# Two attentions and two gated layers in one kernel: where the weights between the attentions are placed, and how much of V and of the gate and up weights stays resident

## The chip, the cores and the metric

The kernel runs on one core of a Trainium2 chip. The metric is device time in microseconds, the median of several executions. One execution more was taken by the hardware profiler; its trace is what the readings below come from.

## The reference

The program computes four layers in a row on a tiny batch: four sequences, one token each, model width 512. Attention A and gated layer B are each applied twice, with the same weights and the same cache both times:

```python
def _A_ref(x, k_cache, v_cache, wq, wo):
    W = min(4096, max(256, Sk // 4))                    # 2048 of 8192 positions
    q = (x @ wq) ...                                    # 32 heads of 128
    k = jnp.repeat(k_cache[:, :, Sk - W:, :], 4, axis=1)   # 8 heads in the cache
    v = jnp.repeat(v_cache[:, :, Sk - W:, :], 4, axis=1)
    p = _softmax(einsum(q, k) * Dh ** -0.5)
    return einsum(p, v) ... @ wo

def _B_ref(x, w_gate, w_up, w_down):
    return (_sigmoid(x @ w_gate) * (x @ w_up)) @ w_down    # 512 -> 1792 -> 512

x = x + _A_ref(_layernorm(x), ...)     # layer 0
x = x + _B_ref(_layernorm(x), ...)     # layer 1
x = x + _A_ref(_layernorm(x), ...)     # layer 2
x = x + _B_ref(_layernorm(x), ...)     # layer 3
```

All arrays are bfloat16. K and V of one cache head (all four sequences, 2048 positions) are 2 MB each, 32 MB for both and all eight heads. The query and output weights are 4 MB each, gate, up and down 1.75 MB each.

## The kernel before

**Memory.** The on-chip memory is counted in *units* of 256 bfloat16 columns, 64 KB over the 128 partitions. K or V of one head is 32 units, a quarter of a gate or up matrix (128 of the 512 rows) is 7 units, the query weights are 64, four blocks of the down weights are 8. There are these buffers: `kt` (K of all heads, 256 units), `wo_sb` (output weights, 64 units, called "ws" in the table of places), `arena` ("ar", 75 units), `side` ("sx", 31 units), and the small `qs`, `pb`, `pt`. K and the output weights are loaded once and serve both attentions. Half of the query weights stays in `side` and at the end of `arena`. V is streamed in both attentions, but the pieces that still lie in `arena` from the first attention are not loaded again: `VKEEP` names, for a head, the first unit of the piece that is kept.

**Places.** The dictionary `WHERE` says for each load where it lands: `V0_h` and `V2_h` are V of head h in the first and second attention, `u01`, `g23_1` and so on pairs of quarters of up and gate (`_1` and `_3` is the layer), `d4_1` the down weights from block 4 on, `q01` the streamed half of the query weights. A load into a place where something else lay waits until the last reader of that has finished. Nothing else holds it back.

**Order.** A planner lists all operations with their data dependences, then orders each engine's by its own list of costs. SyncE (SP) issues all loads, in the order in which the program lists them; one that waits holds up all behind it. The other engines take ready operations, with a preference for those listed first. So when places change, the order of operations on TensorE, VectorE and ScalarE may change with them. The engines wait on one another by semaphores.

**The stages.** In the first attention each head's K is transposed on TensorE (L740), the scores are computed (L763), a maximum over them is taken (L772), exponentials are made on ScalarE (L785), transposed on VectorE (L791) and by a permuting matmul (L796), spread into a block form (L821 on VectorE, L828 on ScalarE), multiplied with V (L863 for a wide form whose partial sums are then added in L879, L921 for a narrow one), selected by row (L961, L968) and multiplied with the output weights (L988). Six TensorE steps, two ScalarE steps and up to nine VectorE steps per head follow one another. The second attention does the same without the transposes of K. It computes scores two heads ahead of the product with V. V of its heads 2 to 7 goes into `kt`, where K of heads 0 to 6 was, as soon as the scores of these heads are done.

Between the attentions stands layer 1: up and gate (L1157), the sigmoid on ScalarE, down (L1233), then the norm and the query projection of layer 2 (L703). Part of the output weights is meanwhile moved into the accumulators ("stash", L1036) and back (L1031), so that `wo_sb` has room for streamed weights. Layer 3 is the same as layer 1 with another form of the down product (L1230); then the output is written.

The quarters of gate and up are multiplied in the order up 0, up 1, gate 0 to 3, up 2, up 3, which `glu` writes out; the blocks of the down weights of layer 1 in the order 0, 4, 7, 8, 10, 12 (the first block of each piece).

Of the kernel before, what the change touches and what calls it, by code (L numbers as in the profile page):

```python
# [268 lines left out]
def build(nc, A_x, A_k, A_v, A_wq, A_wo, B_wg, B_wu, B_wd, out):  # L269
# [4 lines left out]
    _, HKV, SK, DH = A_k.shape  # L274
# [4 lines left out]
    NC = D // 128  # L279
    F = B_wg.shape[1]  # L280
    NFC = F // 128
# [16 lines left out]
    UHEAD = NB * UBLK  # L298
    KEEPG = 4
    GU = F // UNIT  # L300
# [6 lines left out]
    WIDE = {0: {0: 4, 1: 4, 2: 4, 3: 4, 4: 4, 5: 4, 6: 2}, 2: {2: 2, 3: 2, 4: 2, 5: 2}}  # L307
    VKEEP = {0: 24, 7: 19}
    HEADS1 = list(range(1, HKV - 1)) + [0, HKV - 1]
# [29 lines left out]
    with es:  # L339
# [81 lines left out]
        MAIN = WKEEP[2][0][1]  # L421
        G0 = MAIN - KEEPG * GU
# [618 lines left out]

        def load_g(L, nm, ktc, keep):
            key = (nm, ktc // 2, 0 if keep or (nm, ktc // 2, 0) in gkeep else L)
            if key not in gkeep:
                s = WHERE["%s%d%d" % (nm, key[1] * 2, key[1] * 2 + 1) + ("_%d" % L if key[2] else "")]
                gkeep[key] = s
                dma("w%s%d_%d" % (nm, L, ktc), blk_ap(s), (wg_d if nm == "g" else wu_d)[:, key[1], :], w=blk_tok(s),
                    rate="bw_7k")
            s = gkeep[key]
            return (s[0], s[1] + ktc % 2 * GU, GU)  # L1050
# [85 lines left out]
        def glu(L, last_layer):  # L1136
# [9 lines left out]
            wid = NB if last_layer else NB + 1  # L1146
            for nm, ktc in (("u", 0), ("u", 1), ("g", 0), ("g", 1), ("g", 2), ("g", 3), ("u", 2), ("u", 3)):
                bank = GB if nm == "g" else UB
                keep = not last_layer and 2 * ktc + (nm == "u") < KEEPG
                s = load_g(L, nm, ktc, keep)  # L1150

                def e_g(pe, ktc=ktc, s=s, bank=bank):
                    last = None
                    for fc in range(NFC):
                        g0, gn = WD[fc // 4]
                        cols = blk_ap(s)[:, g0 * 128:(g0 + gn) * 128].rearrange("p (m j) -> p j m", j=gn)
                        last = pe.matmul(ps[:, bank, fc * wid:(fc + 1) * wid],  # L1157
                                         cols[:, fc - g0, :],
                                         xn[:, ktc * (NB + 1):ktc * (NB + 1) + wid],
                                         start=(ktc == 0 and fc == 0), stop=(ktc == NC - 1),  # L1160
                                         skip_group_check=True)
# [53 lines left out]
            if not last_layer:  # L1215
                parts[1:] = [(4, 7), (7, 8), (8, 10), (10, 12), (12, 14)]
            for fc0, fc1 in parts:
                s = load_d(L, fc0, fc1)

                def e_d(pe, fc0=fc0, fc1=fc1, s=s):  # L1220
                    last = None
                    src = blk_ap(s)
                    for fc in range(fc0, fc1):
                        for c in range(NC):
# [3 lines left out]
                            if last_layer:  # L1228
                                f0 = fc // 7 * 32 + fc % 7
                                last = pe.matmul(ps[32 * c:32 * c + 25, YB, 0:128], hS[:, f0:f0 + 25], wd,  # L1230
                                                 start=False, stop=(fc == NFC - 1), skip_group_check=True)
                            else:
                                last = pe.matmul(ps[:, YB, c * NB:(c + 1) * NB], wd, hf,  # L1233
                                                 start=(fc == 0 and c == 0), stop=(fc == NFC - 1),
                                                 skip_group_check=True)
# [188 lines left out]
```

## Time and profile before

| what | value |
|---|---|
| time, three executions | 174.51 us median, 174.02 to 175.1 |
| the profiled execution | 174.79 us, of which the profile's span is 173.05 |
| mean granted TensorE clock | 0.82 |
| TensorE busy | 136.2 us, 79% of the span, 2179 matmuls |
| VectorE busy | 100.7 us, 58% |
| ScalarE busy | 77.3 us, 45% |
| read from HBM | 68.62 MB, 397 GB/s over the span |
| first attention, layer 1 and query projection, second attention, layer 3 | to about 106, to 124, to 162, to 173 us |

Times in the profile are microseconds from the start of the span. A row of the timeline has the start, the duration, the engine, the line of the kernel, the operation, the operands as out<-in, their shapes and the count; brackets hold the idle time of the engine ahead of the row and what ended it. "us to landing" of a transfer is counted from its issue by SyncE. Where a text says that a transfer lands at some time, it is the sum of both.

### The profile page before, as it was taken

To read this page: it belongs to the slowest core of one execution; us is meant where nothing else is said; L and a number is where in the kernel's file an instruction comes from. 1 tells how busy PE (TensorE), PEld (TensorE's weight loads), DVE (VectorE), ACT (ScalarE), POOL (GpSimd) and SP (SyncE) were. 2 spreads that over 40 slices of the span, in tenths; PEclk is the share of its full clock that TensorE was granted. 3 is DMA by queue.
4 is the path that set the end of the run, shared out by engine and by line. 5 is a ranking of instruction groups with operands and counts; after the bars stand their busy time and mean duration, and the time that the engine had idled before them with its cause. 6 is when DMAs were issued, how large, how long until landed. Compare 5 with 4: busy or idle time off the path is not lost.

```text
span 173.0 us, 4894 instructions
## 1 busy us (share of the span) xinstructions
PE 136.2 (79%) x2179; PEld 100.4 (58%) x2179; DVE 100.7 (58%) x252; ACT 77.3 (45%) x134; POOL 8.0 (5%) x19
## 2 busy tenths in 40 slices
PE   0395589899898779998979676657977989689883
PEld 0292388658466458565655366546625756458772
DVE  7535015886848675795797653113279877754450
ACT  2064207848576646566291230110767463554200
POOL 5200000000000000000000000202200000000020
PEclk9999756999999987999999755555569999956755
DMA  5999999999999999999999999999999999999960
GB/s 183 424 422 411 432 424 428 439 409 449 424 416 433 400 445 424 412 427 428 420 417 418 397 419 416 406 400 411 386 385 452 426 420 405 424 416 423 407 250 5
DMA packets 9361, 68.93 MB, mean 398 GB/s; under 512 B 1017, under 2 KB 1917, under 8 KB 6013
## 3 DMA queue, kind: packets, MB, share of 16 engines
q1 hardware_dynamic: 9332, 68.62, 95.7%
q8 instruction: 17, 0.28, 0.6%
q14 instruction: 4, 0.02, 0.0%
q10 hardware_dynamic: 8, 0.00, 0.0%
HBM read 68.62 MB, written 0.00 MB: 397 GB/s over the span
## 4 chain that ended last, share of the span: by engine, by line
DMA 65%; PE 23%; DVE 6%; ACT 2%; issue 2%; SPq 1%; DVEq 0%; ACTq 0%
DMA arena<-in_A_v_cache_dram 32%; DMA kt<-in_A_k_cache_dram 12%; DMA kt<-in_A_v_cache_dram 10%; DMA wo_sb<-in_B_w_down_dram 7%; PE ps L863 5%; PE ps L740 4%; DMA wo_sb<-in_A_wq_dram 4%; PE ps L763 3%; PE ps L1157 2%; PE ps L921 2%; SPq L464 1%; DVE pt L821 1%; PE ps L1230 1%; PE ps L836 1%; PE ps L988 1%
## 5 line engine op out<-in xcount | busy, mean ns | idle before, releaser
L750 ACT COPY kt<-ps 128x1024 bf16<-128x1024 bf16 x40 | 39.2, 1017 | 28.2 <-PE ps L740 28.0
L740 PE MATMUL ps<-ident_r,kt 128*128 128x128 bf16 x512 | 40.4, 238 | 5.1 <-DMA kt<-in_A_k_cache_dram 3.1
L740 PEld LDWEIGHTS ps<-ident_r,kt 128*128 128x128 bf16 x512 | 34.9, 109 | 11.8 <-issue 4.4
L750 DVE COPY kt<-ps 128x1024 bf16<-128x1024 bf16 x24 | 29.1, 1214 | 14.2 <-PE ps L740 14.0
L763 PE MATMUL ps<-kt,qs 128*32 128x512 bf16 x256 | 18.3, 413 | 1.2 <-ACT pb L785 1.2
L821 DVE TENSOR_TENSOR pt<-ps,ofbr 128x1024 bf16<-128x1024 f32 (+1 forms) x15 | 15.4, 1029 | 2.7 <-PE ps L796 2.7
L863 PE MATMUL ps<-arena,pt 128*64 128x512 bf16 (+1 forms) x128 | 13.1, 377 | 3.0 <-DMA arena<-in_A_v_cache_dram 3.0
L772 DVE TENSOR_REDUCE nmz<-ps 128x1 f32<-128x512 f32 x16 | 11.0, 688 | 5.9 <-PE ps L763 5.8
L791 DVE STREAM_TRANSPOSE pb<-pb 128x512 bf16<-128x512 bf16 x16 | 11.3, 704 | 4.2 <-ACT pb L785 4.1
L785 ACT ACTIVATE pb<-ps,nmz 128x512 bf16<-128x512 f32 x16 | 11.1, 692 | 5.8 <-DVE nmz L782 5.8
L828 ACT ACTIVATE pt<-ps,ofbr 128x96 bf16<-128x96 f32 x28 | 7.2, 342 | 7.8 <-PE ps L796 7.8
L863 PEld LDWEIGHTS ps<-arena,pt 128*64 128x64 bf16 (+1 forms) x128 | 5.9, 111 | 7.9 <-DMA arena<-in_A_v_cache_dram 4.0
L763 PEld LDWEIGHTS ps<-kt,qs 128*32 128x32 bf16 x256 | 5.8, 101 | 7.8 <-ACT pb L785 2.2
L872 ACT COPY arena<-ps 128x512 f32<-128x512 f32 (+1 forms) x7 | 3.9, 555 | 11.9 <-PE ps L863 11.7
L1031 ACT COPY wo_sb<-ps 128x1024 bf16<-128x1024 bf16 x5 | 5.0, 1011 | 9.1 <-PE ps L703 9.1
L836 PE MATMUL ps<-rowf,nmz 128*128 128x16 f32 x32 | 6.9, 292 | 2.7 <-DVE pt L821 2.5
L836 PEld LDWEIGHTS ps<-rowf,nmz 128*128 128x128 f32 x32 | 5.4, 212 | 5.8 <-DVE pt L821 4.2
L1157 PE MATMUL ps<-xn,arena 128*128 128x5 bf16 (+1 forms) x168 | 6.3, 172 | 2.2 <-DMA arena<-in_B_w_up_dram 1.1
L634 POOL TENSOR_TENSOR rs<-pt,rs 128x4 f32<-128x4 f32 x3 | 3.0, 1014 | 106.0 <-DVE pt L630 106.0
L879 PEld LDWEIGHTS ps<-arena 128*128 128x128 f32 x52 | 6.7, 201 | 2.1 <-ACT arena L872 1.6
L879 PE MATMUL ps<-arena 128*128 128x16 f32 x52 | 7.4, 273 | 0.6
L1157 PEld LDWEIGHTS ps<-xn,arena 128*128 128x128 bf16 x168 | 6.3, 118 | 2.5 <-DMA arena<-in_B_w_up_dram 1.2
(170 smaller groups left out, 162.9 us busy)
## 6 DMA issues: line engine op xcount, KB each, us to landing
kt<-in_A_k_cache_dram SPq DMA_DIRECT2D x8, 2048.0 KB, 24.6
arena<-in_A_v_cache_dram SPq DMA_DIRECT2D x7, 2048.0 KB, 20.2
kt<-in_A_v_cache_dram SPq DMA_DIRECT2D x3, 2048.0 KB, 14.9
wo_sb<-in_A_wo_dram SPq DMA_DIRECT2D x8, 512.0 KB, 25.1
kt<-in_A_v_cache_dram SPq DMA_DIRECT2D x4, 1024.0 KB, 19.3
kt<-in_A_wq_dram SPq DMA_DIRECT2D x1, 2048.0 KB, 11.7
side<-in_A_wq_dram SPq DMA_DIRECT2D x1, 1984.0 KB, 15.8
arena<-in_B_w_up_dram SPq DMA_DIRECT2D x2, 896.0 KB, 8.0
```

The source lines that it names most:

```text
L740: last = pe.transpose(bankb(bank)[:, (v * NB + q) * 128:(v * NB + q + 1) * 128], kt[:, c0:c0 + 128], ident_b[:, :])
L750: return (e.tensor_copy if ev == "vector" else e.copy)(to, fr)
L763: last = pe.matmul(ps[32 * b:32 * b + 32, sbk, 0:CB * 128], qs[:, q0:q0 + 32], blk_ap(kblk(h, b))[:, c * CB * 128:(c + 1) * CB * 128], sta ...
L772: lambda v: v.tensor_reduce(nmv, ps[:, sbk, 0:CB * 128], AXX, ALU.max, negate=True),
L785: o = a.activation(pbuf[:, :], ps[:, sbk, 0:CB * 128], ACTF.Exp, bias=gv, scale=1.0, accum_out=zv)
L791: P.op("vector", "ptr%d_%d" % (L, h), 650.0, lambda v: v.transpose(turned[:, :], pbuf[:, :]), r=[("pb", 0), ("pb", 1)], w=[("pb", 2), ("pb ...
L821: lambda v: v.tensor_tensor(pv4[:, 0:nj], spread(tbk, nj).unsqueeze(2).broadcast_to([128, nj, NB, REP]), ofb[:, :].unsqueeze(1).unsqueeze( ...
L828: last = a.mul(pv4[:, nj:NJ4, b, :], spread(MB, NJ4 - nj), ofb[:, b:b + 1])
L836: lambda pe: pe.matmul(ps[:, tbk, CB * NQ:CB * NQ + NR], zv.broadcast_to([128, 128]), rowf[:, :], start=True, stop=True),
L863: last = pe.matmul(ps[rows * g:rows * (g + 1), bank, 0:wide * 128].rearrange("p (c d) -> p c d", c=wide), ptv[:, w0:w0 + rows], v, start=( ...
L879: last = pe.matmul(ps[:, out[0], out[1]:out[1] + NR], part[:, c * 128:(c + 1) * 128], ey[wide][:, c * NR:(c + 1) * NR], start=(c == 0), st ...
L1157: last = pe.matmul(ps[:, bank, fc * wid:(fc + 1) * wid], cols[:, fc - g0, :], xn[:, ktc * (NB + 1):ktc * (NB + 1) + wid], start=(ktc == 0 ...
```

## The change

The change gives other places to the weights that stand between the attentions, and to what is kept.

- Of V, head 0 keeps 24 units (before 8) and head 7 keeps 15 (before 13), 39 together. Head 0's second attention loads one piece of 8 units into `side`, in place of four pieces. Of gate and up, the quarters up 0, up 1 and gate 1 stay resident (21 units; before also gate 0, 28). Layer 3 loads gate 0 again, as a load of its own.
- In layer 1, up 2 and up 3 are loads of their own. Up 3 is placed where gate 2 was, the first four down blocks where gate 3 was, the down blocks from 6 on where gate 0 was; the streamed query weights are placed where up 2, up 3, down pieces 0 and 4, and down piece 6 with part of gate 0 were. In each case the load waits for TensorE's reading of what lay there.
- The quarters of layer 1 are multiplied in the order up 0, up 1, gate 2, 3, 0, 1, up 2, up 3; the down pieces in the order 4, 8, 0, 10, 12, 6. The loads of pieces 4 and 8 are issued ahead of that of up 3.

```diff
-    KEEPG = 4
+    KEPTG = {("u", 0), ("u", 1), ("g", 1)}
...
-    VKEEP = {0: 24, 7: 19}
+    VKEEP = {0: 8, 7: 17}
...
-        WHERE["V0_%d" % (HKV - 1)] = [ar(0, 19), ar(23, 13)]
-        WHERE["u01"], WHERE["g01"] = ar(52, 2 * GU), ar(38, 2 * GU)
+        WHERE["V0_%d" % (HKV - 1)] = [ar(15, 17), ar(0, 15)]
+        WHERE["u01"], WHERE["g01"] = ar(36, 2 * GU), ar(22, 2 * GU)
         PT3 = ("kt", 187, 4)
         WHERE.update({
-            "g23_1": ("ws", 8, 2 * GU), "u23_1": ar(0, 2 * GU),
-            "d0_1": ar(14, 8), "d4_1": ("ws", 22, 6), "d7_1": ar(36, 2), "d8_1": ("qs", 0, 4), "d10_1": ("pb", 0, 4),
-            "d12_1": ("pt", 4, 4),
-            "q01": [("ws", 8, 10), ar(0, 14), ("ws", 18, 8)],
-            "V2_0": [ar(14, 9), ar(36, 2), sx(0, 8), sx(8, 5), ar(66, 8)],
-            "V2_1": [sx(13, NS - 13), ar(0, 14)],
+            "g23_1": ("ws", 8, 2 * GU), "u2_1": ar(15, GU), "u3_1": ("ws", 8, GU),
+            "d4_1": ("ws", 24, 4), "d8_1": ("qs", 0, 4), "d10_1": ("pb", 0, 4), "d12_1": ("pt", 4, 4),
+            "d0_1": ("ws", 15, 8), "d6_1": ar(22, 4),
+            "q01": [ar(15, 7), ("ws", 8, 7), ("ws", 15, 13), ar(24, 5)],
+            "V2_0": [sx(0, 8), ar(50, 24)],
+            "V2_1": [sx(8, NS - 8), ar(15, 9)],
             "V2_6": [("kt", 128, 16), ("kt", 144, 16)],
-            "V2_7": [("kt", 160, 12), ("kt", 172, 7), ar(23, 13)],
-            "g23_3": ar(0, 2 * GU), "u23_3": sx(0, 2 * GU),
-            "d0_3": ar(14, 8), "d4_3": ("kt", 192, 8), "d8_3": ("kt", 200, 8), "d12_3": sx(14, 4),
+            "V2_7": [("kt", 160, 10), ("kt", 170, 7), ar(0, 15)],
+            "g0_3": ("kt", 0, GU), "g23_3": ar(15, 2 * GU), "u23_3": sx(0, 2 * GU),
+            "d0_3": ("kt", 8, 8), "d4_3": ("kt", 192, 8), "d8_3": ("kt", 200, 8), "d12_3": sx(14, 4),
         })
...
-            for nm, ktc in (("u", 0), ("u", 1), ("g", 0), ("g", 1), ("g", 2), ("g", 3), ("u", 2), ("u", 3)):
+            turn = [("u", 0), ("u", 1)] + [("g", a) for a in ((1, 0, 2, 3) if last_layer else (2, 3, 0, 1))] + [("u", 2), ("u", 3)]
+            early_d = {}
+            for at, (nm, ktc) in enumerate(turn):
...
+                if not last_layer and (nm, ktc) == ("u", 3):
+                    early_d.update((a, load_d(L, a, a + 2)) for a in (4, 8))
...
-                parts[1:] = [(4, 7), (7, 8), (8, 10), (10, 12), (12, 14)]
+                parts = [(4, 6), (8, 10), (0, 4), (10, 12), (12, 14), (6, 8)]
```

On TensorE the new plan moves, in the second attention, the scores of head 7 behind the product of head 4 with V, and the probabilities of head 6 and the partial sums of head 4 ahead of the first half of head 5's product. On the other engines the same operations follow in a like order; on ScalarE the copy of head 5's partial sums comes ahead of the exponentials of head 7 instead of behind them.

More of the change, by code (lines that the diff above doesn't have):

```diff
@@ L421, in build @@
         MAIN = WKEEP[2][0][1]
-        G0 = MAIN - KEEPG * GU
         def ar(u, n):
@@ L1040, in build, with load_g @@
         gkeep = {}
-        def load_g(L, nm, ktc, keep):
-            key = (nm, ktc // 2, 0 if keep or (nm, ktc // 2, 0) in gkeep else L)
+        def load_g(L, nm, ktc):
+            kept = (nm, ktc) in KEPTG
+            name = "%s%d_%d" % (nm, ktc, L)
+            if not kept and name in WHERE:
+                s = WHERE[name]
+                dma("w" + name, blk_ap(s), (wg_d if nm == "g" else wu_d)[:, ktc // 2, ktc % 2 * F:(ktc % 2 + 1) * F], w=blk_tok(s),
+                    rate="bw_4k")
+                return s
+            key = "%s%d%d" % (nm, ktc // 2 * 2, ktc // 2 * 2 + 1) + ("" if ktc < 2 else "_%d" % L)
+            s = WHERE[key]
             if key not in gkeep:
-                s = WHERE["%s%d%d" % (nm, key[1] * 2, key[1] * 2 + 1) + ("_%d" % L if key[2] else "")]
                 gkeep[key] = s
-                dma("w%s%d_%d" % (nm, L, ktc), blk_ap(s), (wg_d if nm == "g" else wu_d)[:, key[1], :], w=blk_tok(s),
-                    rate="bw_7k")
-            s = gkeep[key]
+                dma("w" + key, blk_ap(s), (wg_d if nm == "g" else wu_d)[:, ktc // 2, :], w=blk_tok(s), rate="bw_7k")
             return (s[0], s[1] + ktc % 2 * GU, GU)
@@ L1146, in glu, with e_g @@
             wid = NB if last_layer else NB + 1
-            for nm, ktc in (("u", 0), ("u", 1), ("g", 0), ("g", 1), ("g", 2), ("g", 3), ("u", 2), ("u", 3)):
+            turn = [("u", 0), ("u", 1)] + [("g", a) for a in ((1, 0, 2, 3) if last_layer else (2, 3, 0, 1))] + [("u", 2), ("u", 3)]
+            early_d = {}
+            for at, (nm, ktc) in enumerate(turn):
                 bank = GB if nm == "g" else UB
-                keep = not last_layer and 2 * ktc + (nm == "u") < KEEPG
-                s = load_g(L, nm, ktc, keep)
-                def e_g(pe, ktc=ktc, s=s, bank=bank):
+                first, end = ktc == turn[0 if nm == "u" else 2][1], ktc == turn[-1 if nm == "u" else 5][1]
+                if not last_layer and (nm, ktc) == ("u", 3):
+                    early_d.update((a, load_d(L, a, a + 2)) for a in (4, 8))
+                s = load_g(L, nm, ktc)
+                def e_g(pe, ktc=ktc, s=s, bank=bank, first=first, end=end):
                     last = None
@@ L1159, in e_g @@
                                          xn[:, ktc * (NB + 1):ktc * (NB + 1) + wid],
-                                         start=(ktc == 0 and fc == 0), stop=(ktc == NC - 1),
-                                         skip_group_check=True)
+                                         start=(first and fc == 0), stop=end, skip_group_check=True)
                     return last
@@ L1215, in glu @@
             if not last_layer:
-                parts[1:] = [(4, 7), (7, 8), (8, 10), (10, 12), (12, 14)]
+                parts = [(4, 6), (8, 10), (0, 4), (10, 12), (12, 14), (6, 8)]
             for fc0, fc1 in parts:
-                s = load_d(L, fc0, fc1)
+                s = early_d[fc0] if fc0 in early_d else load_d(L, fc0, fc1)
                 def e_d(pe, fc0=fc0, fc1=fc1, s=s):
@@ L1233, in e_d @@
                                 last = pe.matmul(ps[:, YB, c * NB:(c + 1) * NB], wd, hf,
-                                                 start=(fc == 0 and c == 0), stop=(fc == NFC - 1),
+                                                 start=(fc == parts[0][0] and c == 0), stop=(fc == parts[-1][1] - 1),
                                                  skip_group_check=True)
```

## The prediction

> **What bounds the kernel now.** I read the page's busy lines and slices first, then the chain, the table of windows, the timelines of TensorE and SyncE, and the rows of DMA issues.
>
> The slices of the page:
>
> ```profile
> ## 2 busy tenths in 40 slices
> ...
> PEclk9999756999999987999999755555569999956755
> DMA  5999999999999999999999999999999999999960
> ...
> HBM read 68.62 MB, written 0.00 MB: 397 GB/s over the span
> ## 4 chain that ended last, share of the span: by engine, by line
> DMA 65%; PE 23%; DVE 6%; ACT 2%; issue 2%; SPq 1%; DVEq 0%; ACTq 0%
> ```
>
> The DMA engines are full in every slice but the first and the last two, and 65% of the chain is transfers. So bytes matter. But in order of time the chain leaves the transfers at 149.9 us (V of head 5, first half) and stays on TensorE, VectorE and ScalarE to the end: the last 23 us are computing. Whether fewer bytes shorten the end is therefore decided in the second attention. Its windows:
>
> ```profile
> core 0: us, PE busy (x) PEld busy (x) DVE busy (x) ACT busy (x) POOL busy (x), PEclk, DMA share, GB/s
> ...
> 135.21:138.62 3.41, 3.39 (x91) 2.36 (x79) 2.98 (x12) 1.75 (x7) 0.00 (x0) 1.00 0.97 413
> ...
> 142.03:145.45 3.42, 3.06 (x62) 1.95 (x62) 2.34 (x9) 1.95 (x7) 0.00 (x0) 1.00 0.97 410
> 145.45:148.87 3.42, 3.07 (x64) 1.97 (x63) 3.33 (x11) 1.87 (x7) 0.54 (x2) 1.00 0.99 414
> 148.87:152.28 3.41, 1.96 (x30) 1.46 (x30) 1.90 (x7) 1.52 (x6) 0.00 (x0) 1.00 1.02 425
> 152.28:155.69 3.41, 2.96 (x28) 1.91 (x28) 1.88 (x5) 1.70 (x7) 0.00 (x0) 0.50 0.99 409
> ```
>
> The first figures are the window and TensorE's busy time; the last three are granted clock, DMA share and rate. TensorE is full to about 142, has gaps to 152.3, and then is granted half its clock. The gaps, in TensorE's timeline:
>
> ```profile
> 142.57 1.06 PE L863 MATMUL ps<-kt,pt 128*32 128x256 bf16 x32 [0.36 <-DMA kt<-in_A_v_cache_dram]
> ...
> 147.49 1.06 PE L863 MATMUL ps<-kt,pt 128*32 128x256 bf16 x32 [0.35 <-DMA kt<-in_A_v_cache_dram]
> 148.37 0.39 PE L988 MATMUL ps<-wo_sb,onr 128*16 128x512 bf16 x4
> ...
> 149.99 0.62 PE L863 MATMUL ps<-kt,pt 128*32 128x256 bf16 x16 [0.90 <-DMA kt<-in_A_v_cache_dram]
> ...
> 152.58 0.60 PE L988 MATMUL ps<-wo_sb,onr 128*16 128x512 bf16 x4 [0.32 <-DVE onr L968]
> ```
>
> Three products with V (heads 3, 4 and the first half of 5) wait for their transfer: 0.36 + 0.35 + 0.90 = 1.61 us. Earlier products don't: V of head 2 lands at 125.92 + 11.5 = 137.4 and is used at 139.0. The same output projection takes 0.39 us at full clock and 0.60 after 152.28.
>
> **Bytes.** A unit is 256 columns, 64 KB. Kept V grows from 8 + 13 to 24 + 15 units, so V of head 0 loads 8 instead of 24 and V of head 7 loads 17 instead of 19. Kept gate and up fall from 28 to 21, so the second gated layer loads 7 more. Net 11 units, 0.72 MB. Heads 3 and 4 are issued at 127.63 and 129.41 and land 14.9 and 18.0 later, 142.5 and 147.4: 4.9 us for 32 units, 0.153 each. So from V of head 1 to V of head 6 everything lands 16 × 0.155 = 2.5 us earlier, V of head 7 2.8, and the last down weights 1.75 earlier (150.28 + 18.8 = 169.1 becomes 167.3).
>
> **The weights between the attentions.** Up, gate, down and query weights up to the second attention are 116 units before and after, so the last query weights still land at 116.54 + 6.9 = 123.4 if SyncE's queue never runs dry. This is where waits are added, each on a read by TensorE. SyncE issues in order, so everything later stands behind the waiting load. What counts is the lead: how long after the issue the transfer ahead of it lands. Before:
>
> ```profile
> 95.29 0.54 SPq L464 DMA_DIRECT2D arena<-in_A_v_cache_dram  x1
> ...
> 98.89 0.34 SPq L464 DMA_DIRECT2D arena<-in_B_w_up_dram  x1
> ...
> 116.54 0.33 SPq L464 DMA_DIRECT2D wo_sb<-in_A_wq_dram  x1
> ```
>
> V of head 7 is issued at 95.29 and lands 8.3 later, 103.6; the up weights were issued at 98.89, so their lead is 4.7 us, the smallest there. After the change the leads are:
> - up 0/1 stand where sums of head 0 lay. Those are read until 99.32 + 1.03 = 100.35: lead 3.2.
> - gate 0/1 and up 2 wait for head 7's first 34 products, 103.3; gate 2/3 ahead lands at 108.0: lead 4.7.
> - up 3 takes gate 2's place, read at about 109.4 (TensorE ran 42 such matmuls in 108.26 to 109.75, right behind the norm). Ahead are gate 0/1 (110.2), up 2 (111.3) and two down pieces of 0.7 each (112.7): lead 3.2. Behind it stand all other down pieces and the query weights.
> - the query pieces wait for up 2, up 3, the 8-unit down piece and the last down piece. That last one is read at 118.8, as now (row at 118.42, 0.38 long): leads 3.8 to 5.
> - V of heads 0 and 1 wait for the query matmuls in the side buffer, 119.7 and 121.0: leads 3.7. V of head 2 is issued at 125.9 as now: lead 4.0 instead of 6.6.
>
> A dry queue costs the latency of one transfer less the lead. That latency lies between 2.1 us (the output, issued at 170.92, span end 173.05) and 2.7 (first K, 7.6 us to landing less 4.9 for its bytes). All leads are above 2.7, so I take 0. Bounds: nothing, and, if the two leads of 3.2 fell short by half a microsecond each, +1.0. What hides these waits is the queue's backlog.
>
> The other edits I cost at nothing. The matmuls are the same, only head 0's kept columns come first in its product. From V of head 7 to the output there are 37 issues in both versions. Rows get shorter in places: up 2/3, one load of 14 units with 7 KB rows, becomes two of 7 units with 3.5 KB. The nearest row is V of head 7's second piece, 7 units of 3.5 KB rows, which lands at 142.23 + 18.2 = 160.4, 1.1 us behind its first piece (141.65 + 17.6): 0.16 a unit, as the wide ones. Bounds: nothing to 0.2 for all of them.
>
> **TensorE's path.** Until the product of head 3 nothing waited for V, so it starts at about 142.2 instead of 142.57 whatever lands earlier. From there the order changes: the scores of head 7 (1.05 us at 145.76) move from before the product of head 4 to behind it, and the probabilities of head 6 and the sums of head 4 come before the first half of head 5. With V there, the first half of head 5 ends 1.1 us earlier (if waits for VectorE of 0.3 to 0.5, like those at 151.74 and 152.58, take the place of part of the three) to 1.6 (if none do). I take 1.5, nearer to the row of the three waits, because work that filled no gap now fills them. Next, the second half of head 5 (1.07 at half clock, from 152.97) and its output projection (0.60) would run ahead of 152.28, at 0.55 and 0.39. That is 0.7 less; the exponentials and transposes of head 7 (0.69 + 0.71) are now the partner they wait for, and hide part. I take 0.5; bounds 0, and 1.3 if the busier windows keep the full clock up to the last product as well. Sum on the path: −1.5 − 0.5 = −2.0.
>
> A limit from the transfers: V of head 7 lands at 160.4 − 2.8 = 157.6, and from there to the end of its output projection it takes 162.2 − 160.4 = 1.8, so 159.4. TensorE's path gives 160.2 and decides. Behind it the second gated layer takes 162.2 to 170.9 as now, 8.7 us, and its last down weights (167.3) are there before they are read (168.0 and later). So all of the −2.0 reaches the end.
>
> The span was 173.05 and its run 174.79; after, 171.05 and 172.79. That run is 0.28 above the median of the three, 174.51. Against the median: **172.5 us**.
>
> On the clock, the Trainium skill's page "TensorE: Matmul & The Clock Gate" (Part 1: The HAM clock gate) says that the clock is either half or full, and goes by how busy TensorE was in free-running windows of about 3.4 us. The windows above agree: 1.96 of 3.41 us busy was followed by 0.50, 3.07 by 1.00. By that rule the fuller window at 148.9 would leave the clock at full rate; the rival below prices it from rows.
>
> **The rivals.**
> - The clock falls as before, or a little earlier, and VectorE's chain replaces the waits: only 1.1 is gained, 173.4. For it: the window of 148.87 gets the shorter matmuls too and stays near the limit. Chance 0.26.
> - The clock stays full to the last product. 155.69 to 159.10 was all busy at half clock; without that, and with the −2.0, TensorE would pass the transfers' limit, so the limit holds: 159.4, −2.8, 171.7. Chance 0.14.
> - Transfers are hidden anyway: TensorE at 99% in 135 to 138.6 is the bound, and freed waits turn into waits for VectorE (busy 3.33 of 3.42 in 145.45 to 148.87). Only the 0.36 before head 3 goes: 174.2. Chance 0.08.
> - Slower: the queue runs dry between the attentions. Place: up 3 and the pieces behind it, whose places come free only when TensorE has read them. From the query weights to head 3 computing has no slack, so a delay there reaches the end in full. It decides as soon as 123.4 becomes later than 125.4. With three leads short by 1.2 each, 3.6 − 2.0 = +1.6, 176.1. Against it: leads over 3. Chance 0.10.
>
> My forecast, 171.9 to 172.9, has 0.42.
>
> **How the numbers follow.** About 1% (1.75 us, bound at 172.76) is what a measurement of this kernel can tell from no change. Faster: four fifths of the forecast's 0.42, the full-clock case's 0.14, a tenth of 0.26: 0.50. Slower: 0.10. The rest, 0.40, is within 1%. The range goes from the full-clock case less 0.8 for cheaper transfers, 170.9, to 174.7, which takes in the hidden case and a queue that is dry for two microseconds; beyond lie the rest of the slower case and little else.
>
> **What would show it.** HBM read 67.90 MB. Up 3 issued near 109.4 and no gap of SyncE after which a landing comes over 1 us late. Query weights landed by 123.4, scores of head 0 from 124.0. No wait of L862 on V in the second attention; PE clock full until at least 152. The output issued near 168.9. I am wrong if the scores start later than 125, or if TensorE's gaps before the products stay, now put down to VectorE.

## The result, and the profile after

The changed kernel is slower. Its median is 175.56 us, that of the kernel before in the same session 174.42; the ratio is 1.0068 with a 95% interval of 1.0047 to 1.0090, so 1.2 us more. The forecast was 172.5, in a range of 170.9 to 174.7. The profiled execution took 175.99 us with a span of 174.15.

The slices, the bytes and the chain on the page of the changed kernel:

```profile
PEclk9999855999999999999999855555567899995555
DMA  5999999999999999999999999998999999999960
...
HBM read 67.90 MB, written 0.00 MB: 390 GB/s over the span
## 4 chain that ended last, share of the span: by engine, by line
DMA 48%; PE 31%; DVE 12%; ACT 3%; issue 2%; SPq 1%; DVEq 0%; ACTq 0%
```

The bytes are what was forecast, 0.72 MB fewer. But slice 28 of the DMA row is no longer full, the rate over the span fell from 397 to 390 GB/s, and the transfers' share of the chain fell from 65% to 48%: TensorE's went from 23% to 31% and VectorE's from 6% to 12%. SyncE's issues behind up 3, in its timeline, and two rows of DMA issues (KB, and us from issue to landing) for the last two query pieces:

```profile
109.06 0.33 SPq L463 DMA_DIRECT2D wo_sb<-in_B_w_up_dram  x1
...
115.74 2.04 SPq L463 DMA_DIRECT2D wo_sb<-in_A_wq_dram  x2
118.71 0.33 SPq L463 DMA_DIRECT2D arena<-in_A_wq_dram  x1
```

```profile
wo_sb<-in_A_wq_dram SPq DMA_DIRECT2D x1, 832.0 KB, 6.8
arena<-in_A_wq_dram SPq DMA_DIRECT2D x1, 320.0 KB, 6.4
```

The second row of the timeline is two loads, the second and the third query piece. The third (13 units) had to wait until the down product had read piece 0, and was issued at 117.46. The piece ahead of it landed at 120.45, so its lead was 2.99 us. It landed at 117.46 + 6.8 = 124.28, which is 3.83 behind the piece ahead; 13 units need 2.05 at the rate of full slices. So 1.8 us of transfers were lost there. The last piece landed at 125.08 (before 123.41). The windows show the hole, first in the changed kernel, then in the kernel before:

```profile
core 0: us, PE busy (x) PEld busy (x) DVE busy (x) ACT busy (x) POOL busy (x), PEclk, DMA share, GB/s
...
118.00:120.00 2.00, 1.47 (x49) 1.34 (x47) 0.88 (x5) 0.00 (x0) 0.10 (x1) 0.50 0.89 249
120.00:122.00 2.00, 1.89 (x57) 1.80 (x54) 1.07 (x6) 0.00 (x0) 0.36 (x2) 0.50 0.80 310
122.00:124.00 2.00, 0.36 (x14) 0.27 (x11) 0.00 (x0) 1.01 (x1) 0.85 (x1) 0.50 0.92 327
```

```profile
118.00:120.00 2.00, 1.45 (x49) 1.28 (x46) 0.88 (x5) 0.00 (x0) 0.55 (x1) 0.50 1.00 408
120.00:122.00 2.00, 1.89 (x57) 1.81 (x55) 1.06 (x6) 0.00 (x0) 0.26 (x2) 0.50 1.03 409
122.00:124.00 2.00, 1.64 (x57) 1.51 (x57) 0.49 (x2) 1.69 (x2) 0.94 (x1) 0.50 1.04 369
```

The last column is the rate, the one ahead of it the DMA engines' busy share. I call *hole* what is short of 410 GB/s over the five windows of 2 us from 116 to 126, in us of transfer: 2.0 after, 0.2 before. The difference, 1.8 us, is as much as 0.72 MB take (1.75). The saving was spent before the second attention began. A hole is not all idle time: by the shares of the three windows (0.89, 0.80, 0.92 against 1.00 to 1.04) the engines stood idle for about 0.9 us of it, and in the rest they were busy with packets that took longer, by their records in the trace: those of the third query piece took up to 2.1 us each, where the median was 0.25. TensorE's timeline of the changed kernel, and then two rows of the kernel before:

```profile
115.10 0.61 PE L1165 MATMUL ps<-xn,wo_sb 128*128 128x5 bf16 x14 [3.04 <-DMA wo_sb<-in_B_w_up_dram]
...
124.33 0.85 PE L702 MATMUL ps<-xn,wo_sb 128*128 128x4 bf16 x26 [1.97 <-DMA wo_sb<-in_A_wq_dram]
...
125.96 3.56 PE L762 MATMUL ps<-kt,qs 128*32 128x512 bf16 x32 [0.41 <-DVE pt L715]
...
133.35 1.90 PE L762 MATMUL ps<-kt,qs 128*32 128x512 bf16 x16 [0.51 <-ACT pb L784]
...
144.38 0.83 PE L762 MATMUL ps<-kt,qs 128*32 128x512 bf16 x12 [1.10 <-issue]
```

```profile
123.46 0.59 PE L703 MATMUL ps<-xn,wo_sb 128*128 128x4 bf16 x16 [0.36 <-DMA wo_sb<-in_A_wq_dram]
123.98 3.60 PE L763 MATMUL ps<-kt,qs 128*32 128x512 bf16 x32
```

In the changed kernel it waits 3.04 us for up 3 (which makes the down product, and so the third query piece, late), then 1.97 us for that query piece. The scores of head 0 start at 125.96 (before 123.98). The scores of head 3 run at half clock (1.90 instead of 1.05), and within those of head 5 there is a stall of 1.10. None of the products of L862 waits for V. The output is issued at 172.01, before 170.92.

A second profiled execution of each kernel was taken to see what of this is of the kernel.

> The changed kernel once more, for a second profiled execution. What belongs to the kernel comes again: up 3 issued near 109, the third query piece issued near 117.5 and landing after 123.8, the scores of head 0 at 125.5 to 126.5, no wait for V before head 6. If the half clock at the scores of head 3 (1.90 us instead of 1.05) and the stall of 1.10 us inside the scores of head 5 belong to it too, the output is issued near 172; if they are chance of one execution, one or both are missing and it is issued near 170.5 to 171.2.

> The kernel before once more, for a second profiled execution: scores of head 0 at 123.9 to 124.5, V of head 2 landing near 137.5, of head 7 near 160.4, waits of TensorE for V ahead of the products of heads 3, 4 and 5 of 1.0 to 1.8 us together, and the output issued at 170.2 to 170.9 (the median run is 0.5 us shorter than the profiled one).

The changed kernel took 175.91. Third query piece issued at 117.77 with a lead of 3.02, last query weights at 126.13, scores at 126.53, half clock at the scores of head 3 again, output issued at 172.03. The stall inside head 5's scores did not come again, and yet the output was no earlier. V of head 7 landed at 161.38, and its output projection ended 1.73 behind that, the same step from transfers to the end as the 1.8 of before. In the first execution V of head 7 had landed at 160.72 and the projection ended 3.11 behind it: there computing was the later of the two. The kernel before took 174.50: scores at 123.89, V of head 7 at 160.47, waits for V of 0.33 and 0.88, output at 170.53.

### The profile page after: what moved, and what is told of

Read it like the earlier page. It is cut to its first block, busy times and chain, and to the rows that moved or that the text cites. A ratio compares the mean times of both kernels' runs of the same rounds, so it can differ in the third digit from the quotient of the medians.

```text
span 174.1 us, 4894 instructions
## 1 busy us (share of the span) xinstructions
PE 134.4 (77%) x2179; PEld 99.4 (57%) x2179; DVE 101.0 (58%) x252; ACT 77.2 (44%) x134; POOL 8.0 (5%) x19
## 3 DMA queue, kind: packets, MB, share of 16 engines
q1 hardware_dynamic: 9332, 67.90, 95.1%
HBM read 67.90 MB, written 0.00 MB: 390 GB/s over the span
## 4 chain that ended last, share of the span: by engine, by line
DMA 48%; PE 31%; DVE 12%; ACT 3%; issue 2%; SPq 1%; DVEq 0%; ACTq 0%
DMA arena<-in_A_v_cache_dram 29%; DMA kt<-in_A_k_cache_dram 12%; PE ps L762 6%; PE ps L862 5%; PE ps L739 5%; DMA wo_sb<-in_A_wq_dram 4%; PE ps L920 4%; PE ps L1165 3%; DMA wo_sb<-in_B_w_up_dram 3%; DVE pt L820 2%; DVE nmz L771 2%; DVE pb L790 2%; ACT pb L784 2%; SPq L463 1%; DVE kt L749 1%
## 5 line engine op out<-in xcount | busy, mean ns | idle before, releaser
L739 PE MATMUL ps<-ident_r,kt 128*128 128x128 bf16 x512 | 39.8, 237 | 5.3 <-DMA kt<-in_A_k_cache_dram 3.2
L739 PEld LDWEIGHTS ps<-ident_r,kt 128*128 128x128 bf16 x512 | 34.1, 108 | 12.1 <-issue 3.6
L762 PE MATMUL ps<-kt,qs 128*32 128x512 bf16 x256 | 19.6, 434 | 2.8 <-ACT pb L784 1.3
L862 PE MATMUL ps<-arena,pt 128*64 128x512 bf16 (+1 forms) x128 | 12.6, 355 | 3.6 <-DMA arena<-in_A_v_cache_dram 3.6
L862 PEld LDWEIGHTS ps<-arena,pt 128*64 128x64 bf16 (+1 forms) x128 | 5.7, 106 | 8.4 <-DMA arena<-in_A_v_cache_dram 4.6
L1165 PE MATMUL ps<-xn,arena 128*128 128x5 bf16 (+1 forms) x140 | 5.7, 173 | 2.0 <-DMA arena<-in_B_w_gate_dram 0.8
L1165 PEld LDWEIGHTS ps<-xn,arena 128*128 128x128 bf16 x140 | 5.5, 118 | 2.4 <-issue 0.9
```

The costliest lines, as they stand in the source:

```text
L739: last = pe.transpose(bankb(bank)[:, (v * NB + q) * 128:(v * NB + q + 1) * 128], kt[:, c0:c0 + 128], ident_b[:, :])
L762: last = pe.matmul(ps[32 * b:32 * b + 32, sbk, 0:CB * 128], qs[:, q0:q0 + 32], blk_ap(kblk(h, b))[:, c * CB * 128:(c + 1) * CB * 128], sta ...
L862: last = pe.matmul(ps[rows * g:rows * (g + 1), bank, 0:wide * 128].rearrange("p (c d) -> p c d", c=wide), ptv[:, w0:w0 + rows], v, start=( ...
L1165: last = pe.matmul(ps[:, bank, fc * wid:(fc + 1) * wid], cols[:, fc - g0, :], xn[:, ktc * (NB + 1):ktc * (NB + 1) + wid], start=(first and ...
```

## The experiments

Theory 1 was the dry queue: the new places make loads wait for a TensorE that is itself late, and the hole delays all that follows. The rivals: the new order of the engines in the second attention costs it; or saved bytes bring nothing in any case. Ratios are to the kernel before, with their intervals. Where units of kept V are overwritten or V is not loaded, the expectation says which.

**Taking the late weights away.** Three kernels free one wait or both, by using units of kept V as places.

```diff
-            "q01": [ar(15, 7), ("ws", 8, 7), ("ws", 15, 13), ar(24, 5)],
+            "q01": [ar(15, 7), ("ws", 8, 7), ar(50, 13), ar(24, 5)],
```

> The changed kernel, but the third piece of query weights of the second attention (13 units) is loaded onto units of kept V of head 0, which nothing reads in between, in place of the room of the second down piece; the bytes and the order on every engine stay. (Head 0's product of the second attention then reads query weights for 13 of its 32 units, and adds what stands there.) Theory 1, the dry queue: the piece no longer waits for the late down product, is issued near 116.1 instead of 117.46 and lands near 122.5 instead of 124.28; the last piece lands near 123.5 instead of 125.08, the scores of head 0 start between 124.0 and 124.5 instead of 125.96, and the time is 1.5 to 2 us below the changed kernel's, 173.5 to 174.0. Rival 2, the new order in the second attention (clock, stalls) costs it: the scores start as early, but the time stays within 0.4 of the changed kernel's 175.6. Rival 3, the transfers set the end and start late elsewhere: query weights stay at 125.

```diff
-            "g23_1": ("ws", 8, 2 * GU), "u2_1": ar(15, GU), "u3_1": ("ws", 8, GU),
+            "g23_1": ("ws", 8, 2 * GU), "u2_1": ar(15, GU), "u3_1": ar(50, GU),
...
+                s = load_g(L, nm, ktc)
                 if not last_layer and (nm, ktc) == ("u", 3):
                     early_d.update((a, load_d(L, a, a + 2)) for a in (4, 8))
-                s = load_g(L, nm, ktc)
```

> The changed kernel, but up 3 of the first gated layer is loaded onto units of kept V of head 0 and ahead of the two early down pieces, so that it waits for no read of gate 2. (Head 0's product of the second attention then reads up weights for 7 of its 32 units.) Theory 1: up 3 lands near 112.5 to 113.8 instead of 115.05, TensorE's wait of 3.04 us for it shrinks to under 1.8, the third query piece is issued near 116.2 instead of 117.46 because the down product comes earlier, and of the 2.0 us by which the second attention starts late 1.0 to 2.0 come back: 173.6 to 174.6. Rival 2 (the order in the second attention): time within 0.4 of 175.6 though the scores start earlier. A second rival within theory 1, that only the missing lead of the query piece matters and not up 3: the query piece is still issued after 117 and nothing is gained.

> Both edits together: up 3 early on units of kept V and the third query piece on the 13 units behind it. (Head 0's product of the second attention then reads up and query weights for 20 of its 32 units.) Theory 1: no landing between the attentions is more than 0.5 us late, query weights at 123.0 to 123.5, scores of head 0 from 123.6 to 124.2, and what is left is what fewer bytes bring by themselves: 173.0 to 173.6, that is 0.8 to 1.4 below the kernel before. Forecast of the prediction without its failed lead: 172.5. Rival 2: 175 or more. Rival 3, fewer bytes bring nothing: 174.2 to 174.6, as before.

The ratios: 1.0025 (1.0002 to 1.0048), 1.0068 (1.0044 to 1.0091), 1.0043 (1.0022 to 1.0064). The first gives back 0.7 us of the 1.2. None gets below the kernel before: their medians are 174.60, 175.17 and 174.87, the kernel's before 174.08, and theory 1 had 174.6 at the most. In the first and the third the scores were still late, at 124.92 and 125.60 (expected: 124.5 and 124.2 at the latest), since the last query piece, which still waited for a down product, landed at 124.51 and 125.19; their holes are 1.4 and 1.1 us. The second taught most. TensorE in it:

```profile
124.13 3.60 PE L762 MATMUL ps<-kt,qs 128*32 128x512 bf16 x32 [0.42 <-DVE pt L715]
...
143.63 1.06 PE L862 MATMUL ps<-kt,pt 128*32 128x256 bf16 x32 [0.92 <-DMA kt<-in_A_v_cache_dram]
...
148.55 1.06 PE L862 MATMUL ps<-kt,pt 128*32 128x256 bf16 x32 [1.59 <-DMA kt<-in_A_v_cache_dram]
```

The scores are on time (124.13), and yet the time is that of the changed kernel. Now TensorE waits 2.51 us for V, and V of head 7 lands at 161.16, before 160.40, with 0.72 MB fewer to move. (This execution took 176.77, 1.6 above its median, and V of head 3 came 6.4 us behind V of head 2 instead of 4.9: 15 of its 16 parts, one for each DMA engine, had landed by 141.32, the last at 143.59. So its waits are larger than usual.) V of head 2 landed at 137.17, against 136.92 in the changed kernel and 137.47 before. So the late start of computing is not all of it: V comes hardly earlier either.

A kernel with both of the last query pieces on kept units:

```diff
-            "q01": [ar(15, 7), ("ws", 8, 7), ("ws", 15, 13), ar(24, 5)],
+            "q01": [ar(15, 7), ("ws", 8, 7), ar(50, 13), ar(63, 5)],
```

> The changed kernel with the third and the fourth piece of query weights on kept units of V of head 0, so that no query weight waits for a down product (head 0's product then reads query weights for 18 of its 32 units). Bytes as in the changed kernel. Theory A: query weights land by 123.8, the scores of head 0 start at 124.0 to 124.4, which takes the delay away; the queue then runs dry behind them, where V waits for the side buffer, V of head 2 lands near 137 as in all the others, and the time is that of the kernel before within 0.5: a ratio of 0.999 to 1.003. Rival, the saved bytes show once the query weights are on time: a ratio of 0.993 or less.

Scores at 124.48, V of head 2 at 136.89, ratio 1.0047 (1.0026 to 1.0068), a little above the range. The rate now falls in another place, 122 to 126 (323 and 327 GB/s), where V waits for `side`; the hole is 1.5 us.

A part of what is missing in these kernels lies behind the second attention. In the profiled executions of the first, the third and this one the output projection of head 7 ended at 161.46, 161.93 and 161.74, before at 162.19 and 162.07. But from there to the output it took 9.4, 9.4 and 9.1 us, before 8.7 and 8.5. Two rows of the first one's TensorE in layer 3, with stalls for which the trace shows no wait ("issue"):

```profile
162.84 0.98 PE L1165 MATMUL ps<-xn,arena 128*128 128x4 bf16 x26 [0.89 <-issue]
...
169.00 1.25 PE L1237 MATMUL ps<-kt,pt 128*25 128x128 bf16 x39 [0.55 <-issue]
```

The kernel before has 0.24 and 0.52 there, in its second execution none and 0.52. No run tests what makes these stalls.

**The saving by itself.** The kernel before, without the first two pieces of V of head 0 (11 units):

```diff
+                if L == 2 and h == 0 and u0 in (0, 9):
+                    got.append((s, u0 * UNIT // 128))
+                    u0 += n
+                    continue
```

> The kernel before, with its places and its order, but the first two pieces of V of head 0 in the second attention (11 units, 0.72 MB, as many bytes as the change saves) are not loaded; the product reads what lies there. This is the saving alone, without the new places. Forecast of the prediction: V of heads 2 to 6 lands about 1.7 earlier, TensorE's three waits for V (1.6 us) go, and the time falls by 1.0 to 2.0 to 172.4 to 173.4. Rival 3, transfers are hidden anyway: 174.2 to 174.6. The scores of head 0 stay at 124.0 in either.

Ratio 1.0023 (1.0000 to 1.0046): nothing gained. V of head 2 landed at 137.32 instead of 137.47. But here the planner had also given the second attention another order (the scores of head 7 behind the product of head 4, as in the changed kernel). Two more kept the order of before on every engine, one with 9 units fewer at the same place, one with 11 units fewer behind the stretch, in V of head 2:

```diff
+                m = n - 11 if L == 2 and h == 2 else n
+                t = (s[0], s[1], m)
-                dma("V%d_%d_%d" % (L, h, u0), blk_ap(s), v_d[h][:, :, u0 * UNIT:(u0 + n) * UNIT], w=blk_tok(s),
+                dma("V%d_%d_%d" % (L, h, u0), blk_ap(t), v_d[h][:, :, u0 * UNIT:(u0 + m) * UNIT], w=blk_tok(s),
```

(For the 9 units: `m = 1 if L == 2 and h == 0 and u0 < 11 else n`.)

> The kernel before, every engine in its old order, but of the first two pieces of V of head 0 in the second attention (9 and 2 units) only one unit each is loaded: 9 units less (0.59 MB, 1.4 us of transfers), ahead of the loads that wait for places in the side buffer. Unlike the run that left out both pieces, the order on every engine is that of before. Theory A: the rate falls under 330 GB/s around 120 to 126, V of head 2 lands at 137.0 to 137.5 as before (137.47), the waits for V stay, and the time is within 0.4 of the kernel before. Rival, it was the new order on the engines that ate the gain there: V of head 2 lands near 136.1 and the time is 0.8 to 1.5 below the kernel before.

> The kernel before, every engine in its old order, but the last 11 units of V of head 2 in the second attention are not loaded (0.72 MB, the saving of the change and of the run with less V of head 0; the product reads what lies there). Now the bytes are missing behind the stretch between the attentions, where the loads stand 10 us and more ahead of their landing. Theory A, the place of the saving decides: saved bytes shorten nothing where the next loads wait for places that TensorE frees, and count in full where the queue is deep. Then V of heads 3 to 6 lands 1.5 to 1.7 us earlier (head 3 near 140.9, first half of head 5 near 148.3), TensorE's three waits for V (1.61 us) fall to under 0.5, and the time is 1.0 to 1.8 below the kernel before: 172.3 to 173.1. Theory B, the end is bound by computing (clock, VectorE, the tail) whatever V does: V lands earlier, but the time stays within 0.4 of the kernel before, 173.7 to 174.5.

Early: 0.9974 (0.9949 to 0.9999). Deep: 0.9956 (0.9936 to 0.9977). The windows of the early one:

```profile
120.00:122.00 2.00, 1.90 (x57) 1.81 (x55) 1.12 (x7) 0.00 (x0) 0.20 (x1) 0.50 0.83 292
122.00:124.00 2.00, 1.61 (x56) 1.52 (x56) 0.54 (x3) 1.28 (x2) 1.01 (x1) 0.50 1.18 346
124.00:126.00 2.00, 2.00 (x32) 0.98 (x34) 0.60 (x3) 1.97 (x3) 0.00 (x0) 0.50 0.90 309
```

The hole is there, 1.4 us (before 0.2), where 9 units take 1.4: with the loads gone that had been the cover, nothing could be issued until TensorE had read the weights in `side`. But V of head 2 still landed 1.0 earlier (136.50), so "shorten nothing" was too strong: the saving is worth 0.45 us, and the rival had 0.8 to 1.5. In the deep one the hole is 0.4 and V of head 7 lands at 159.13, and it is worth 0.77. The intervals overlap, so that a saving is worth more behind the stretch than in it is likely, not shown. In neither does a product of L865 wait for V; in the early one that of the last head does, 0.26. What is left on TensorE's path are waits for VectorE (0.52 and 0.32 at 151 to 153, as before). With V out of the way the kernel ends 0.4 to 0.8 us earlier, not 2.0.

**Filling the hole.**

```diff
+            if u0 == 14:
+                dma("again", blk_ap(ar(50, 11)), v_d[0][:, :, 8 * UNIT:19 * UNIT], w=blk_tok(ar(50, 11)), rate="bw_4k",
+                    nbytes=128 * 11 * UNIT * 2)
             dma("wq2_%d" % u0, blk_ap(w),
```

> The changed kernel, which loads 11 units more (0.72 MB): the kept columns 8 to 18 of V of head 0 once again, onto the same place, issued right ahead of the third query piece, that is just ahead of the hole in the queue. All results stay. Theory A: the bytes fill the hole, the third query piece lands at 124.2 to 124.8 instead of 124.28, and the time is within 0.4 of the changed kernel's ratio of 1.007 to the kernel before: the 0.72 MB that the change saves are worth nothing there. Rival, bytes count wherever they are: 1.3 to 1.7 us slower than the changed kernel, a ratio of 1.015 to 1.017.

Ratio 1.0105 (1.0072 to 1.0139), between the two: 0.65 us more than the changed kernel for 1.75 us of bytes. The third query piece landed at 125.41, where 124.8 at the latest was expected. By difference about 1.1 of the 1.75 went into the hole; the interval of the ratio leaves 0.5 to 1.7. With all bytes loaded the new places and the new order thus cost 1.8 us together.

**Adding the suspected wait to the kernel before**, and nothing else:

```diff
         order = _schedule(P.ops, tm)
+        late = dict((o.name, o) for o in P.ops)
+        late["wq2_24"].deps.add(late["glu_d1_12"])
```

> The kernel before with all its bytes, places and its order on every engine, but its last query piece (8 units, now issued at 116.54 with a lead of 5.6 us) waits also for the last down product, and so is issued near 118.9 with a lead of 3.1 to 3.3 us; the loads of V stand behind it. This adds the suspected wait alone. Theory, a lead of 3 us counted to the slowest of the 16 engines is too short: the piece lands 0.8 to 1.8 us later than 123.41, the scores of head 0 start at 124.7 to 125.8, and the time is 0.5 to 1.5 us above the kernel before, a ratio of 1.003 to 1.009. Rival, what the prediction took (a queue is dry only when the lead is under 2.7 us): the piece lands at 123.4, ratio 0.999 to 1.002.

Ratio 1.0114 (1.0073 to 1.0156): 2.0 us, the largest of all. But not by the way expected. Its windows, and TensorE:

```profile
118.00:120.00 2.00, 1.44 (x48) 1.36 (x48) 0.88 (x5) 0.00 (x0) 0.42 (x1) 0.50 0.68 271
120.00:122.00 2.00, 1.89 (x56) 1.81 (x52) 1.06 (x6) 0.00 (x0) 0.39 (x2) 0.50 0.93 273
122.00:124.00 2.00, 1.49 (x53) 1.39 (x53) 0.49 (x2) 1.82 (x2) 0.81 (x1) 0.50 0.97 319
124.00:126.00 2.00, 2.00 (x21) 0.82 (x24) 0.58 (x3) 1.97 (x3) 0.00 (x0) 0.50 0.93 296
```

```profile
123.95 3.41 PE L763 MATMUL ps<-kt,qs 128*32 128x512 bf16 x32
...
148.87 1.06 PE L863 MATMUL ps<-kt,pt 128*32 128x256 bf16 x32 [0.28 <-DMA kt<-in_A_v_cache_dram]
...
151.34 0.62 PE L863 MATMUL ps<-kt,pt 128*32 128x256 bf16 x16 [0.88 <-DMA kt<-in_A_v_cache_dram]
```

The query piece was issued at 118.69 with a lead of 3.27 and landed at 123.39, as early as before; the scores start on time. But the rate is down from 118 on. The parts of the piece ahead ended on the 16 engines from 118.77 to 121.97, so that the first engine was done 0.07 us behind the issue of the query piece. From last to last there is hardly a gap: 1.42 us for 8 units, which take 1.26. The hole of 2.3 us falls on V behind it: V of head 2 lands at 139.04 (137.47), of head 7 at 161.87 (160.40), and V is waited for as before, later.

**Through what does the hole reach the end?** By now both TensorE's start and the landing of V had shown as ways. Two runs took 11 units of V of head 2 away behind the hole, from the changed kernel and from the one with the added wait (the edit is the one of the deep saving):

> The changed kernel, every engine in its order, but the last 11 units of V of head 2 in the second attention are not loaded (0.72 MB less again; the product reads what lies there). These bytes are missing where the queue is deep, behind the late query weights, which stay late. Theory T, transfers pay: the holes of the queue between the attentions (TensorE late, weights late) cost because V and the last weights land later, and the saved bytes are what is short; then everything from V of head 3 on lands 1.5 to 1.7 us earlier than in the changed kernel and the time falls by 0.8 to 1.5 us: a ratio of 0.998 to 1.002. Theory P, the late start of the scores pays: TensorE has no slack from there to the end whatever V does, the time stays within 0.4 us of the changed kernel, a ratio of 1.005 to 1.009.

> The kernel before in its old order with both edits: its last query piece waits for the last down product too (which alone made a ratio of 1.0114), and the last 11 units of V of head 2 are not loaded (which alone made 0.9956). Theory T, transfers pay: V lands about as in the kernel before (the hole costs 1.6 us, the missing bytes give 1.7), and the time is that of the kernel before within 0.5, a ratio of 0.998 to 1.003. If the late start of computing were what the wait costs, the two edits would not meet in the transfers: 1.007 to 1.011.

Ratios 1.0022 (0.9994 to 1.0050) and 1.0009 (0.9985 to 1.0033). In both the time follows the transfers: the saved bytes take back 0.8 of the changed kernel's 1.2 us, though its scores still start late, at 125.59, and nearly all of the 2.0 of the added wait. For the added wait that is over twice what the same saving brought alone (0.77), so its cost went through the transfers for the most part. For the changed kernel 0.8 is no more than that saving brings anyway: the run speaks against theory P (1.005 or more), but does not show that V is all through which the hole costs. TensorE in the second of them, the scores of head 0 and the one wait for V behind them:

```profile
124.72 3.60 PE L765 MATMUL ps<-kt,qs 128*32 128x512 bf16 x32
...
159.14 0.82 PE L923 MATMUL ps<-kt 128*128 128x32 bf16 x24 [0.21 <-DMA kt<-in_A_v_cache_dram]
```

There is no wait for V any more up to the last head, at 159.14.

**The order of the engines.** The operations of the second attention on TensorE, VectorE and ScalarE were put into the turn that the planner had given the other kernel, by their names:

```diff
         order = _schedule(P.ops, tm)
+        for e, turn in (("tensor", "S2_0 ... WO2_7"), ("vector", "smax2_0 ... omul2_7"), ("scalar", "sexp2_0 ... pta2_7")):
+            turn = turn.split()
+            at = [i for i, o in enumerate(order[e]) if o.name in turn]
...
+            for i, o in zip(at, [by[n].pop(0) for n in turn]):
+                order[e][i] = o
```

> The kernel before, with all its places, loads and bytes, but TensorE, VectorE and ScalarE do their work of the second attention in the turn that the planner gave them in the changed kernel (the scores of head 7 behind the product of head 4, the product of head 5 behind the sums of head 4, and so on). Theory C, the new turn itself costs: the run that left out 11 units of V with a new turn took 0.9 us more than the one that left out 9 in the old turn, so here 0.5 to 1.0 us more than the kernel before, a ratio of 1.003 to 1.006; TensorE's last transposes of probabilities (head 7) come later than 154.24 and the product of head 7 waits for them. Rival, the turn is free: within 0.3 us of the kernel before, 0.998 to 1.002.

> The changed kernel, with its places, loads and bytes, but TensorE, VectorE and ScalarE do the work of the second attention in the turn of the kernel before. Theory C with the late query weights: the ratio falls from 1.007 to 1.001 to 1.004; the scores of head 0 still start near 126. Rival, the late query weights are all of it: 1.005 or more, as the changed kernel.

> The changed kernel with both undone: the third query piece on units of kept V of head 0 (head 0's product then reads query weights for 13 of its 32 units), and the second attention in the turn of the kernel before. What is left is the saving of 0.72 MB. If late weights and the new turn are all that stood against it, the ratio is 0.994 to 0.998, like the two runs of the kernel before with less V (0.9956 and 0.9974). If something else of the change costs, 1.000 or more.

The kernel before with the new turn: 1.0048 (1.0027 to 1.0070), 0.8 us as expected, and the last transposes of probabilities start at 155.50 instead of 153.97. Two lines of its TensorE:

```profile
147.63 1.06 PE L863 MATMUL ps<-kt,pt 128*32 128x256 bf16 x32 [0.49 <-DMA kt<-in_A_v_cache_dram]
...
152.59 0.62 PE L863 MATMUL ps<-kt,pt 128*32 128x256 bf16 x16 [0.30 <-DMA kt<-in_A_v_cache_dram]
```

The last wait for V stands ahead of the second half of head 5's product (in the old turn ahead of the first), and the waits for V come to 0.79 instead of 1.61 us; but the scores of head 7 end at 150.13 instead of 146.81, and the exponentials and transposes behind them are late. The other way round failed. The changed kernel with the old turn: 1.0078 (1.0050 to 1.0106), not 1.001 to 1.004; with the query piece freed as well, 1.0032 (1.0004 to 1.0060), not 0.994 to 0.998. So the turn is no share of the loss that could be taken off. Forced on the kernel before it costs 0.8; taken from the changed kernel it brings nothing. Why the last kernel, with scores at 124.48, V of head 7 at 158.86 and the old turn, is still 0.3% above the kernel before is not settled; its hole is 1.1 us, and its output projection of head 7 ended 3.38 behind V of head 7, so computing was the later there.

No run points to a version that beats both kernels: the two that were faster than before leave loads out.

## Why the prediction was wrong

- **Bytes.** 67.90 MB as forecast. That V of heads 1 to 6 lands 2.5 us earlier failed: V of head 2 landed 0.55 earlier (136.92), the second half of head 6 0.65 later (158.04), the last down weights 1.5 later (170.53). Besides the hole there is a loss behind it: from the landing of V of head 2 to that of V of head 6, the same 128 units in both kernels, it took 21.1 us instead of 19.9 (20.5 and 19.9 in the second executions). No run tests why.
- **The weights between the attentions: "All leads above 2.7, so I take 0".** This is the term that failed. The lead of the third query piece was 2.99, not 3.8 to 5, mostly because up 3 came 1.3 late and TensorE with it (with up 3 early, and down pieces that landed late, it was 3.53), and that cost 1.8 us of transfers. Up 3 was late on one DMA engine alone: 15 of its 16 parts had landed by 113.78, about the forecast (112.7 for the piece ahead and 1.1 for its own seven units), and the last at 115.05. Just ahead, from 111.88, a packet of 16 KB on the queue that the profile calls "instruction" took 1.09 us. In the kernel before such a packet at 112.65 is followed by a like delay (a down piece: 113.67 for the 15th part, 115.00 for the last), and in both second executions too; that the packet held the engine fits these times, no run tests it. In the changed kernel TensorE waits for just this load, and the query pieces wait for TensorE.
- **The rule itself** was wrong too. I counted the lead to the landing of the transfer ahead, which is that of the slowest of 16 DMA engines. The records of the single engines in the trace say that the piece ahead was done on the first engine at 118.41 and on the last at 120.45: for the first the lead was 0.95. In the run with the added wait a lead of 3.27 was 0.07 for the first engine, and the hole was 2.3 us, with nothing else changed. The Trainium skill says on its page "DMA: Bandwidth & Descriptors" (Why a DMA increments its semaphore by 16 and not by 1) that the engines of one DMA finish independently and that the semaphore counts them; the trace agrees, with 2.0 us between first and last here.
- **The rival on the slower side** named the place (up 3 and the pieces behind it) and the mechanism, at a chance of 0.10. Its threshold, query weights later than 125.4, was not reached in the first execution (125.08) and was in the second (126.13); the kernel was slower in both, because the 2.0 us that it set against it were not there. The forecast with a hole of 1.8 is 174.3, and with 0.45 to 0.77 in place of the 2.0 it is 175.5 to 175.9, where 175.56 was measured. That is a sum of two runs' figures and not a proof: it takes the new order and the stalls of layer 3 at nothing.
- **TensorE's path, −2.0.** The three waits for V did go, as said. Of the −2.0, the deep saving in the old order brought 0.77, the early one 0.45. I had taken the waits as a sum on the path, though what ends next behind them stands less than a microsecond away. The waits for VectorE that remain (0.52, 0.32) point to its chain, which was the reason of the first rival, with −1.1.
- **The new order "nothing to 0.2".** Put on the kernel before, it cost 0.8.
- **"From the query weights to head 3 computing has no slack"** was right for TensorE. But with the scores on time (up 3 early) the time was the same, and V of head 2 hardly earlier than before. In one execution of the changed kernel computing ended last, in the other the transfers (3.11 and 1.73 us from V of head 7 to the end of its projection): the two stand close together, and the hole moves both.
- **The clock** was full from 136.17 to 156.65 (asked: at least 152), but stood at half from 132.75 to 136.17, which the prediction did not have. The output was forecast at 168.9 and was issued at 172.01.

## What to carry to other kernels

Count a load's lead from the first DMA engine that finishes the transfer ahead, not from its landing, and allow for the releasing engine to be late; here a lead of 3 us to the landing cost 1.8 us of transfers. Bytes that are taken out just ahead of loads that wait for places leave a hole nearly of their own size (1.2 us more hole for 1.4 us of bytes here), so look for savings where the queue is deep. And where a planner orders the engines, run an edit once with the old order held: a saving of the same kind measured −0.45 us in the old order and +0.4 in the new one.

## What the runs showed of the hardware

- The parts of one transfer on the 16 DMA engines end far apart: 2.0 us in the piece above, 3.4 us (120.20 to 123.57) for the last query piece in the run without V's first pieces. One engine can be late by itself: up 3 in the changed kernel landed 1.27 us behind its 15th part, a down piece in the kernel before 1.33 us.
- The half clock at the scores of head 3 came in both executions of the changed kernel, in neither of the kernel before, and in some of the variants (the deep saving: yes; the early one: no). These scores took 0.85 us longer by it. The busy share of the window before does not decide it alone: TensorE was busy 0.51 of that window in the changed kernel and half clock followed; in the changed kernel with the old turn it was 0.51 too, and the clock stayed full.
- TensorE stalled without a wait ("issue") at the first matmuls of layer 3 (L1165, L1157) for 0 to 1.19 us. How long differed from kernel to kernel, and from one execution to the next (0.23 and 0.66 in the changed kernel); no cause of it was tested.
